# Held stores and a tick given out two parts per step, in a retention block with a gated feed-forward network

## The chip, the cores and the metric

The kernel runs on one core of a Trainium2 chip. The metric is the device time of one execution in microseconds (us); lower is better.

## The reference

```python
def reference(q, k, v, moe_w_gate, moe_w_val, moe_w_out):
    # q, k, v: (8, 8, 576, 64) float32; gates and values 512 x 1536, out 1536 x 512
    scores = (1 / np.sqrt(64)) * np.matmul(q, k.transpose(0, 1, 3, 2))
    gamma = 1.0 - 2.0 ** (-5.0 - np.arange(8))
    rel = pos[:, None] - pos[None, :]
    Dmat = np.where(rel >= 0, gamma[:, None, None] ** rel[None], 0.0)
    attn = np.matmul(scores * Dmat[None], v)
    x = attn.transpose(0, 2, 1, 3).reshape(4608, 512)      # tokens x (heads * 64)
    g = x @ w_gate
    return (g * (1.0 / (1.0 + np.exp(-g))) * (x @ w_val)) @ w_out
```

Everything is float32.

## The kernel before, in words

**The attention part** works on 32 pairs of heads (8 batches, 4 pairs each), in chunks of 128 positions with a running state. A pair passes through three *ticks*: tick t transposes q and k of pair t, computes scores and new states of pair t - 1, and the values of pair t - 2. `tick(t)` (L498 on) puts its matmuls out at once: new states (`mix`, L428, of v and the scaled k), own values (`xo`, L421), earlier values (L433, L438), scores (L444 and L447, of `qT` and `kT`). The rest goes into the list `pieces`, in this order: `keys`, which scales k by the decay of its position on ScalarE (two instructions, L408); `both`, which empties `mix` and `xo` into the activations x (L484, L478); three masked parts (L454 twice, and L459 to L462 together); two transposes on VectorE (L404, `qT` and then `kT`); and, in the later tiles, `next_load(t)`, which issues the load of pair t + 2. `go_on(n)` puts out the next n pieces. A tick first puts out whatever is left of the one before. `kT` and `ret` have one buffer, `qT` and the raw q and k have two, k in its natural order (`kn`) three, v four.

A load of a later pair is 14 transfers on SyncE's queue: four of q and four of k (L278), two of `kn` and two of v (L259), two of the last rows of v (L285). All transfers of the program share eight completion semaphores in turn, so that a transfer is issued only when the one eight places before it has landed.

**The feed-forward part** takes tokens in tiles of 1024 (the first has 512). The first tile uses plain matmuls: `up0(f)` for 12 blocks of hidden units, then `down0(f)` for the same 12 in the order of `down_order`, each four matmuls into four banks (L544). From the second tile on, the products go by a scheme with sums of weights, sums of activations and sums of results: each quarter has 26 products (`N`), in the order of the tables `UP` and `DOWN`. The second tile has 78 up steps (three quarters `qd` of 26), then 26 down steps; the same for the third, fourth and fifth tile.

The sums of the output weights are made once by GpSimd (L563 to L570) while the first tile runs: `out_sums` cuts the list `OUT_SUMS` into groups of three operands, 27 groups in all for three quarters. Each operand is stored to DRAM (L620, `dn<-rest`) by a transfer on SyncE's queue, or, for a group that is called `late`, on ScalarE's. Of late stores up to three wait in the list `waiting` before the oldest is put out:

```python
waiting.append((place.get(slot), lambda: queue.dma_start(...)))
stores_until(3 if late else 0)
```

A store whose operand is a plain piece of the weights has no place of its own (`None`), and `stores_until` then puts out all that wait. The groups of `up0(11)` (three) and of the first four down0 steps (one, one, one, two) are late. Sums have 18 places in SBUF, used again in turn.

In the down0 loop each step puts out its matmuls, `go_on(4)`, perhaps a tick (tick 10 after the second step, 11 after the fourth, 12 after the seventh, 13 after the ninth), and then its groups. Tick 13 is put out whole; ticks 10, 11 and 12 leave their pieces to later steps. Before the second tile, `out0` empties the four banks (VectorE copies A, B and C, L551), with sums of activations (L570 on VectorE) before and after.

In an up step of the second tile (`up_step` with `n == 1`, called `busy`): GpSimd makes sums of up weights for later steps (L570, and L733 after a negation on ScalarE, L732); eight matmuls go into a bank (L763); ScalarE's queue stores the operand for the later tiles (L766, `up<-arena`); at `i == 22` of the first two quarters `first_sums` makes the sums that the next quarter starts with, one of them on VectorE; at `i == 22` of the last quarter three fetches of stored down operands go out on SyncE's queue (L665, `arena<-dn`), and five more at `i == 25`; then `reads` empties the bank (ScalarE copies, L701; VectorE sums, L704; silu on ScalarE, L778; products on VectorE, L781 and L784); then `go_on(1)`. A bank is written again some three steps after it was filled.

The order on every engine and queue is the order of the calls. `merge` spreads ticks over steps: the first 26 up steps of the second tile run without ticks (two loads are put out among them), ticks 12 to 17 lie among the other 52 up steps, 8 or 9 steps each, and ticks 18 to 21 among the 26 down steps (L802), where `go_on(3)` follows each step.

Of the kernel before, what the change touches and what calls it, by code (L numbers as in the profile page):

```python
# [22 lines left out]
def tables(gamma, scale, P, D):  # L23
# [77 lines left out]
OUT_SUMS = [  # L101
    "14 | 10: add 8 4 5, add 9 2 3, nad 10 8 9",
    "2 | 11: add 11 0 1",
    "9 | 5: ",
    "19 | 9: neg 9 9",
    "15 | 12: sub 12 3 7",
    "0 | 11: sub 11 11 8",
    "1 | 13: sub 13 1 5",
    "6 | 10: add 10 0 2",
# [40 lines left out]
def kernel(  # L150
# [236 lines left out]
    def transposes(i):  # L387
        p = i % HP
        qk, kn, vt, last = loaded.pop(i)
        qT = qp.tile([P, S], F32, tag="qT", name="qT")  # L390
        st[i] = dict(qT=qT, kn=kn, v=vt, last=last)
        pieces = []
        if i < HP:

            for t, src, bank in ((qT, qk[0], bankA), (kT, kn, bankB)):
                for c in range(NFULL):
                    nc.tensor.transpose(bank[:, ts(c, P)], src[:, c].rearrange("p h d -> p (h d)"), ident)
                nc.scalar.copy(out=t[:, 0:CW], in_=bank)
            nc.tensor.transpose(bankC[:, 0:P], qk[1].rearrange("p h d -> p (h d)"), ident)
            for n, t in enumerate((qT, kT)):  # L400
                nc.scalar.copy(out=t[:, CW:S], in_=bankC[:, n * REM : (n + 1) * REM])
        else:
            for n, t in enumerate((qT, kT)):
                pieces.append(lambda n=n, t=t: nc.vector.transpose(out=t, in_=qk[:, n].rearrange("p j d -> p (j d)")))  # L404

        def keys():
            for hl in range(2):
                nc.scalar.activation(out=kn[:, :, hl, :], in_=kn[:, :, hl, :], func=AF.Copy,  # L408
                                     scale=key[:, 2 * p + hl : 2 * p + hl + 1])
            if i < RAWS:  # L410
                load_w(i)

        return [keys] + pieces
# [84 lines left out]
    def tick(t, lo=HP, hi=NP, spread=False, then=None):  # L498
        go_on(len(pieces))
        for fn, i in ((new_states, t - 1), (own_values, t - 2), (earlier_values, t - 2), (scores, t - 1)):  # L500
            if lo <= i < hi:
                fn(i)
        new = transposes(t) if lo <= t < hi else []
        pieces.extend(new[:1])
        if lo <= t - 2 < hi:
            pieces.extend(to_x(t - 2))
        if lo <= t - 1 < hi:
            pieces.extend(masked(t - 1))
        pieces.extend(new[1:])
        if then:  # L510
            pieces.append(then)
        if not spread:
            go_on(len(pieces))

    def go_on(n):
        for _ in range(min(n, len(pieces))):
            pieces.pop(0)()

    def needed(n):

        last = (min(starts[n] + TW, NT) - 1) // S
        return last * HP + HP - 1 + 3
# [55 lines left out]
    more_places = [rest[:, raw_at + TB * i : raw_at + TB * (i + 1)] for i in range(16) if i % 4]  # L578

    waiting = []  # L580

    def stores_until(left, place=None):
        while len(waiting) > left or any(p is place for p, _ in waiting):
            waiting.pop(0)[1]()
# [8 lines left out]
    def out_sums(qd):  # L593

        place = {}

        def view(s):
            return w_dn[:, qd, s // 2, s % 2] if s < 8 else place[s]

        def used(e):  # L600
            return [e[1]] if e[0] is None else [int(a) for a in e[1][2:]]

        def release(k):

            for s in list(place):
                for e in events[k + 1 :]:
                    if s in used(e):
                        break
                    if s == e[0]:
                        sum_places.append(place.pop(s))  # L610
                        break
                else:
                    sum_places.append(place.pop(s))

        def do(k, late):
            e = events[k]
            if e[0] is None:
                _, slot, i = e
                src, queue = view(slot), nc.scalar if late else nc.sync
                waiting.append((place.get(slot), lambda: queue.dma_start(out=dn_ops[i][:, qd * TB : (qd + 1) * TB], in_=src)))  # L620
                stores_until(3 if late else 0)
            else:
                new = sum_places.pop(0)
                stores_until(3, new)
                add(nc.gpsimd, e[1], view, new)
                if e[0] in place:
                    sum_places.append(place[e[0]])
                place[e[0]] = new
            release(k)

        r, ends = [], [k for k, e in enumerate(events) if e[0] is None]
        for g in range(0, N, 3):
            lo, hi = ends[g - 1] + 1 if g else 0, ends[min(g + 2, N - 1)] + 1

            def group(late=False, lo=lo, hi=hi):
                for k in range(lo, hi):
                    do(k, late)

            r.append(group)
        return r  # L640

    def up_view(qd):
        return lambda s: (w_up[:, qd, :, s // 2, s % 2, :] if s < 8
                          else extra[:, s - 8].rearrange("p (g x) -> p g x", g=2))
# [25 lines left out]
    def operand():  # L670
        m = used[0]
        used[0] += 1
        return ring[:, (m + 5) % 8]
# [46 lines left out]
    def x_sums(n, lo, hi, vector):  # L720
        for op in x_ops[lo:hi]:
            add(nc.vector if vector or op[0] == "nad" else nc.gpsimd, op, x_view(n))
# [24 lines left out]
    def up_step(n, qd, i):  # L747
        label, opens, xslot, _, wslot, _, ops = up[i]
        busy = n == 1
        if qd == 0:  # L750
            first = X_FIRST_OF_ALL if busy else X_FIRST
            x_sums(n, first + i, first + i + 1, busy)
        if busy:
            if i > 1:
                w_sums(qd, i)
            w = up_view(qd)(wslot)
        else:
            w = operand()[:, 0:512].rearrange("p (g x) -> p g x", g=2)
        rhs = x_view(n)(xslot)
        b = bank(label, i == 0)  # L760
        for gv in range(2):
            for c in range(2):
                nc.tensor.matmul(b[:, gv * TB : (gv + 1) * TB], w[:, gv, ts(c, P)], rhs[:, c, :],  # L763
                                 start=(opens and gv == 0 and c == 0), stop=(c == 1), skip_group_check=True)
        if busy:
            nc.scalar.dma_start(out=up_ops[qd][i].rearrange("p (g x) -> p g x", g=2), in_=w)  # L766
            if i == 22 and qd + 1 < NQ:
                first_sums(qd + 1)
            if qd + 1 == NQ and i >= 22:
                for _ in range(3 if i == 22 else 5 if i == N - 1 else 0):  # L770
                    fetch()
        else:
            fetch()

        def result(o, src, negative, vector):
            s = io[:, (silus[0] % 4) * TB : (silus[0] % 4 + 1) * TB]
            silus[0] += 1
            nc.scalar.activation(out=s, in_=src[:, 0:TB], func=AF.Silu, scale=-1.0 if negative else 1.0)  # L778
            dst = hid[:, qd, o // 4, o % 4]
            if negative:  # L780
                return lambda: nc.vector.scalar_tensor_tensor(out=dst, in0=src[:, TB : 2 * TB], scalar=-1.0, in1=s,  # L781
                                                              op0=ALU.mult, op1=ALU.mult)
            if vector:
                return lambda: nc.vector.tensor_tensor(out=dst, in0=src[:, TB : 2 * TB], in1=s, op=ALU.mult)  # L784
            nc.gpsimd.tensor_tensor(out=dst, in0=src[:, TB : 2 * TB], in1=s, op=ALU.mult)  # L785

        reads(ops, b, busy, result)
        if qd + 1 == NQ and i + 1 == N:
            while products:
                products.pop(0)[1]()  # L790
        go_on(1)

    def down_step(n, i):
        label, opens, slot, hops, ops = down[i]
# [50 lines left out]
    def next_load(t):  # L845
        if t + AHEAD < NP:
            load(t + AHEAD)
# [31 lines left out]
    for m, f in enumerate(down_order):  # L879
        down0(f)  # L880
        if m == 0:
            next_load(9)
        go_on(4)
        if m in tick_at:
            tick(tick_at[m], HP, FIRST, tick_at[m] + 1 < needed(1))
        if m == 8:
            first_sums(0)
        if m > 8:
            x_sums(1, 3 * (m - 9), min(3 * (m - 8), X_FIRST), True)
        for _ in range(min(1 if m < 3 else 2, len(groups))):  # L890
            groups.pop(0)[1](m < 4)
# [52 lines left out]
```

## Time and profile before

| what | value |
|---|---|
| median of 4 runs | 1112.57 us (1110.38 to 1117.3) |
| the profiled execution | 1112.69 us, span of its instructions 1111.0 us |
| TensorE (PE) busy | 1078.7 us, 97% |
| VectorE (DVE) busy | 653.2 us, 59% |
| GpSimd (POOL) busy | 404.6 us, 36% |
| ScalarE (ACT) busy | 257.8 us, 23% |
| mean granted TensorE clock | 0.992 |
| up0 and down0 of the first tile | up to 206 us of the span |
| up steps of the second tile | 206 to 366 us |

A line of the profile gives the kernel's line, the engine, the operation and what it writes and reads; `ACTq` and `SPq` are the queues on which ScalarE and SyncE issue transfers. In brackets stands how long the engine was idle before, and what ended the wait. A list of waits gives for each pair of waiting and awaited instruction the total in us, the number of times and the longest. In a table by stage each row is a stretch of time: its length, the busy time of PE, of PE's weight loads, DVE, ACT and POOL (with the number of instructions), the granted clock of TensorE, the busy share of the transfer engines and their GB/s.

### The profile page before, as it was taken

To read this page: it belongs to the slowest core of one execution; us is meant where nothing else is said; L and a number is where in the kernel's file an instruction comes from. 1 tells how busy PE (TensorE), PEld (TensorE's weight loads), DVE (VectorE), ACT (ScalarE), POOL (GpSimd) and SP (SyncE) were. 2 spreads that over 40 slices of the span, in tenths; PEclk is the share of its full clock that TensorE was granted. 3 is DMA by queue.
4 is the path that set the end of the run, shared out by engine and by line. 5 is a ranking of instruction groups with operands and counts; after the bars stand their busy time and mean duration, and the time that the engine had idled before them with its cause. 6 is when DMAs were issued, how large, how long until landed. Compare 5 with 4: busy or idle time off the path is not lost.

```text
span 1111.0 us, 17302 instructions
## 1 busy us (share of the span) xinstructions
PE 1078.7 (97%) x6372; PEld 884.5 (80%) x6372; DVE 653.2 (59%) x1063; ACT 257.8 (23%) x528; POOL 404.6 (36%) x355
## 2 busy tenths in 40 slices
PE   5999989999999899999999999999999999999998
PEld 4545446788878788888888888888888888888887
DVE  2698962976767765744536767444447455243654
ACT  3454500224232201112221110231321011322210
POOL 1002469366445402552214106622133176222504
PEclk9999999999999999999999999999999999999999
DMA  9989966656566877667467667654564555555653
GB/s 227 222 216 240 235 177 184 186 177 184 147 173 183 234 177 225 194 174 192 125 177 220 162 177 189 192 154 130 151 186 139 158 172 152 153 152 154 189 161 101
DMA packets 304196, 198.31 MB, mean 179 GB/s; under 512 B 219632, under 2 KB 247280, under 8 KB 304112
## 3 DMA queue, kind: packets, MB, share of 16 engines
q1 hardware_dynamic: 272512, 152.80, 53.2%
q10 hardware_dynamic: 31600, 44.41, 12.1%
q8 instruction: 51, 0.84, 0.3%
q14 instruction: 33, 0.27, 0.1%
HBM read 157.04 MB, written 40.11 MB: 177 GB/s over the span
## 4 chain that ended last, share of the span: by engine, by line
PE 79%; DVE 7%; DMA 5%; issue 3%; POOL 3%; ACT 2%; SPq 1%; ACTq 0%; DVEq 0%; POOLq 0%
PE bankE L763 11%; PE bankA L763 11%; PE bankC L763 10%; PE bankB L763 10%; PE bankE L802 6%; PE bankB L802 6%; PE bankC L802 6%; PE bankA L802 6%; PE sc L447 2%; DMA up<-arena 2%; PE xo L421 2%; PE xo L438 1%; DVE rest L373 1%; PE mix L428 1%; DVE rest L704 1%
## 5 line engine op out<-in xcount | busy, mean ns | idle before, releaser
L704 POOL TENSOR_TENSOR rest<-rest 128x512 f32<-128x512 f32 x56 | 79.1, 1417 | 313.8 <-DVE rest L704 288.7
L778 ACT ACTIVATE io<-rest 128x256 f32<-128x256 f32 x180 | 75.0, 417 | 357.0 <-DVE rest L704 311.0
L763 PE MATMUL bankC<-rest,arena 128*128 128x256 f32 x544 | 129.2, 380 | 0.5 <-DVE rest L704 0.5
L763 PE MATMUL bankA<-rest,arena 128*128 128x256 f32 x544 | 128.7, 379 | 0.0
L570 POOL TENSOR_TENSOR arena<-arena 128x512 f32<-128x512 f32 (+1 forms) x72 | 113.4, 1588 | 41.4 <-DMA up<-arena 30.6
L570 POOL TENSOR_TENSOR rest<-rest 128x256 f32<-128x256 f32 (+1 forms) x86 | 81.8, 972 | 122.4 <-DVE rest L375 94.0
L763 PE MATMUL bankE<-rest,arena 128*128 128x256 f32 x512 | 123.0, 384 | 0.0
L763 PE MATMUL bankB<-rest,arena 128*128 128x256 f32 x512 | 121.4, 380 | 0.8 <-DVE arena L781 0.8
L763 PEld LDWEIGHTS bankC<-rest,arena 128*128 128x128 f32 x544 | 102.8, 190 | 15.8 <-issue 1.3
L763 PEld LDWEIGHTS bankA<-rest,arena 128*128 128x128 f32 x544 | 103.2, 190 | 14.6 <-issue 0.5
L785 POOL TENSOR_TENSOR arena<-rest,io 128x256 f32<-128x256 f32 x72 | 51.8, 725 | 172.7 <-ACT io L778 172.7
L763 PEld LDWEIGHTS bankE<-rest,arena 128*128 128x128 f32 x512 | 98.0, 192 | 14.2 <-DVE rest L704 0.4
L763 PEld LDWEIGHTS bankB<-rest,arena 128*128 128x128 f32 x512 | 97.0, 190 | 14.8 <-DVE arena L781 1.2
L704 DVE TENSOR_TENSOR rest<-bankC,rest 128x512 f32<-128x512 f32 x72 | 48.9, 687 | 75.5 <-PE bankC L763 53.4
L704 DVE TENSOR_TENSOR rest<-bankE,rest 128x512 f32<-128x512 f32 x72 | 48.9, 687 | 75.0 <-PE bankE L763 56.0
L704 DVE TENSOR_TENSOR rest<-bankB,rest 128x512 f32<-128x512 f32 x72 | 48.8, 686 | 71.9 <-PE bankB L763 55.3
L704 DVE TENSOR_TENSOR rest<-bankA,rest 128x512 f32<-128x512 f32 x72 | 48.9, 687 | 67.2 <-PE bankA L763 48.9
L781 DVE SCALAR_TENSOR_TENSOR arena<-rest,io 128x256 f32<-128x256 f32 x84 | 55.2, 662 | 11.7 <-ACT io L778 11.7
L802 PE MATMUL bankB<-arena 128*128 128x256 f32 x252 | 58.2, 381 | 0.0
L802 PE MATMUL bankA<-arena 128*128 128x256 f32 x252 | 58.1, 380 | 0.0
L802 PE MATMUL bankC<-arena 128*128 128x256 f32 x252 | 58.0, 380 | 0.0
L802 PE MATMUL bankE<-arena 128*128 128x256 f32 x252 | 57.9, 379 | 0.0
(149 smaller groups left out, 1660.8 us busy)
## 6 DMA issues: line engine op xcount, KB each, us to landing
arena<-up SPq DMA_DIRECT2D x234, 256.0 KB, 2.7
arena<-dn SPq DMA_DIRECT2D x104, 384.0 KB, 3.5
up<-arena ACTq DMA_DIRECT2D x78, 256.0 KB, 2.7
out_dram<-rest SPq DMA_DIRECT2D x32, 256.0 KB, 3.5
qk<-in_q_dram SPq DMA_DIRECT2D x112, 72.0 KB, 3.2
qk<-in_k_dram SPq DMA_DIRECT2D x112, 72.0 KB, 3.1
v<-in_v_dram SPq DMA_DIRECT2D x62, 128.0 KB, 3.1
kn<-in_k_dram SPq DMA_DIRECT2D x58, 128.0 KB, 3.1
```

The costliest lines, as they stand in the source:

```text
L373: nc.vector.scalar_tensor_tensor(out=top, in0=top, scalar=-(1 << 31), in1=dst, op0=ALU.bitwise_and, op1=ALU.bitwise_or)
L421: nc.tensor.matmul(xo[half[hl], ts(c, P)], s["v"][:, c, hl, :], ret[:, hl, ts(c, P)], start=(c == 0), stop=(c == 0), skip_group_check=True)
L428: nc.tensor.matmul(z[half[hl], c], s["kn"][:, c, hl, :], s["v"][:, c, hl, :], start=True, stop=True)
L438: nc.tensor.matmul(o[half[hl]], state[half[hl], c - 1, :], s["qT"][half[hl], c * P : c * P + w], start=False, stop=True, skip_group_check= ...
L447: nc.tensor.matmul(sc[hl][:, ts(c, P)], kT[half[hl], ts(c, P)], qT[half[hl], ts(c, P)], start=True, stop=True)
L570: eng.tensor_tensor(out=dst, in0=srcs[0], in1=srcs[1], op=ALU.add if op[0] == "add" else ALU.subtract)
L704: eng.tensor_tensor(out=at(op[1]), in0=at(op[2]), in1=at(op[3]), op=ALU.add if op[0] == "add" else ALU.subtract)
L763: nc.tensor.matmul(b[:, gv * TB : (gv + 1) * TB], w[:, gv, ts(c, P)], rhs[:, c, :], start=(opens and gv == 0 and c == 0), stop=(c == 1), s ...
L778: nc.scalar.activation(out=s, in_=src[:, 0:TB], func=AF.Silu, scale=-1.0 if negative else 1.0)
L781: return lambda: nc.vector.scalar_tensor_tensor(out=dst, in0=src[:, TB : 2 * TB], scalar=-1.0, in1=s, op0=ALU.mult, op1=ALU.mult)
L785: nc.gpsimd.tensor_tensor(out=dst, in0=src[:, TB : 2 * TB], in1=s, op=ALU.mult)
L802: nc.tensor.matmul(b[:, m * TB : (m + 1) * TB], lhs[:, qd, ts(m, P)], w[:, qd], start=(opens and qd == 0 and m == 0), stop=(qd == NQ - 1), ...
```

## The change

Four edits. The number of late stores that may wait is no longer 3 but a variable that starts at 26; after the second down0 step and its tick it becomes 3 and the surplus is put out. After a tick in the down0 loop, one piece is put out at once: for ticks 10 and 11 that is the scaling of k, for tick 12 the emptying of `xo`; tick 13 has nothing left. In the up steps of the second tile two pieces are put out after each step instead of one. No instruction is added or removed.

```diff
@@ -578,6 +578,7 @@
     waiting = []
+    behind = [len(OUT_SUMS)]
 
     def stores_until(left, place=None):
@@ -618,10 +619,10 @@
                 waiting.append((place.get(slot), lambda: queue.dma_start(out=dn_ops[i][:, qd * TB : (qd + 1) * TB], in_=src)))
-                stores_until(3 if late else 0)
+                stores_until(behind[0] if late else 0)
             else:
                 new = sum_places.pop(0)
-                stores_until(3, new)
+                stores_until(behind[0], new)
                 add(nc.gpsimd, e[1], view, new)
@@ -788,7 +789,7 @@
             while products:
                 products.pop(0)[1]()
-        go_on(1)
+        go_on(2 if busy else 1)
 
     def down_step(n, i):
@@ -883,6 +884,11 @@
         go_on(4)
         if m in tick_at:
             tick(tick_at[m], HP, FIRST, tick_at[m] + 1 < needed(1))
+            go_on(1)
+        if m == 1:
+
+            behind[0] = 3
+            stores_until(3)
         if m == 8:
             first_sums(0)
```

## The prediction

> **What bounds the kernel now.** The page's first part is read first, to see whether any engine is full; then the list of TensorE's waits from 150 to 400 us, which is the stretch that the diff touches.
>
> ```profile
> PE 1078.7 (97%) x6372; PEld 884.5 (80%) x6372; DVE 653.2 (59%) x1063; ACT 257.8 (23%) x528; POOL 404.6 (36%) x355
> ...
> PE bankB L802 <- DMA arena<-dn: 4.1, 1, 4.1
> PE mix L428 <- ACT kn L408: 3.4, 1, 3.4
> PE mix L444 <- DVE kT L404: 2.4, 1, 2.4
> PE bankB L763 <- DVE arena L781: 0.8, 1, 0.8
> PE bankC L763 <- DVE rest L704: 0.5, 1, 0.5
> ```
>
> TensorE (PE) carries the span and stands still in few places: these five waits are 11.2 us. After 386 us it is never idle for more than a pipeline gap, so the change can move the end only through what it does to this list. The timelines of ScalarE (ACT), VectorE (DVE) and SyncE's queue (SP) show what stands before the three long waits, and the table by stage what follows them:
>
> ```profile
> 155.78 9.52 ACTq L620 DMA_DIRECT2D dn<-rest  x13
> 165.34 0.51 ACT L408 ACTIVATE kn<-kn,tab 128x256 f32<-128x256 f32 x1 [26.18 <-DMA qk<-in_k_dram]
> ...
> 303.13 1.74 DVE L570 TENSOR_TENSOR arena<-arena 128x512 f32<-128x512 f32 x1 [1.20 <-POOL arena L733]
> ...
> 309.23 0.76 DVE L404 STREAM_TRANSPOSE kT<-qk 128x576 f32<-128x576 f32 x1
> 310.05 0.33 PE L444 MATMUL mix<-qT,kT 64*64 64x64 f32 x4 [2.38 <-DVE kT L404]
> 311.44 3.60 PE L763 MATMUL bankE<-rest,arena 128*128 128x256 f32 x8
> ...
> 362.37 2.91 SPq L665 DMA_DIRECT2D arena<-dn  x3
> 369.87 3.42 SPq L278 DMA_DIRECT2D qk<-in_q_dram  x4
> 378.93 4.34 SPq L665 DMA_DIRECT2D arena<-dn  x8
> ```
> ```profile
> 165.91:172.34 6.43, 6.43 (x73) 5.75 (x73) 0.89 (x3) 0.34 (x1) 6.19 (x9) 0.58 0.58 174
> 182.84:186.57 3.73, 3.73 (x74) 3.37 (x73) 0.89 (x3) 0.00 (x0) 3.56 (x6) 1.00 0.59 194
> ```
>
> First, the k scaling of tick 10 (L408) stands behind 13 stores on ACT's queue; those wait for GpSimd (POOL), which makes the sums one by one from 152.61. TensorE, free at 162.48, waits 3.42 us, and tick 11 then takes 6.43 us at a granted clock of 0.58, where tick 12 takes 3.73 at 1.00. Second, the k transpose at 309.23 stands behind a weight sum that waited for POOL until 303.13, with multiplications after it. Third, eight fetches (L665) stand behind a load on SP (369.87 to 378.83).
>
> **The change part by part.** The sum is made against the profiled execution: 1112.69 us, of which the span is 1111.0. The median of the runs, 1112.57, lies 0.12 below it.
>
> *Held stores and scaling at once (down0 loop).* No arithmetic is added. By OUT_SUMS only the first three late stores still go out ahead of tick 10 (the third has no place of its own and pushes the two before it). The other ten of the 13 in the fence now stand behind the two scalings of tick 10. The three need a POOL sum that ends at 156.4, so the scaling runs near 158, and TensorE wants it at 162.48: wait gone, with 4 us of margin. Worth 3.42 + (6.43 - 3.73) = 6.1 us. The ten are paced by POOL and lose about 1 us.
>
> At tick 11 eight stores fall behind two scalings that wait for k of pair 11 (before: scaling ended at 176.70). Queued behind them are only these stores and, at 176.61 before, two weight negations that the second tile needs at 200. A store 0.5 us after another from 177.2, landing 2.1 us later, frees its place at 179.3; POOL writes that place again at 180.7. So POOL doesn't wait; without that margin it would, by a microsecond, and TensorE has 10 us of room for POOL's sums.
>
> What is late next? TensorE reaches tick 12 at 182.84 - 6.12 = 176.72. If the load of pair 11 keeps its times, its last v transfer (issued at 175.0, 3.1 to land) costs 1.4 us. But SP's waits show this load held 14.2 us by landings of those same stores; the last eight must now follow the scaling that needs the load, so the load can't wait for them any more. I take 0, and 1.4 as the other end. Then comes the second tile, wanted at 206.09 - 6.12 = 199.97, when bank A must have been copied out by DVE (done at 205.62, margin 0.47). Ahead of the copy stand nine sums: 0.69 us each alone, 1.64 (twice) beside a POOL instruction. POOL's chain doesn't move and runs until about 198, so four or five of the nine become slow instead of three: from 190.5 the copy ends at 200.9 or 201.9, a return of 0.9 to 1.9 (0 if none is slowed more). I take 1.4. Net: -4.7 us.
>
> The Trainium skill ("SBUF — State Buffer", "SBUF: two separate sides") speaks against the change here: the shared port is locked for a whole instruction. By it each overlapped sum would last up to 1.58 + 0.69 = 2.27 us, an estimate by which the return is 2.2; the row's 1.64 is less.
>
> *Two parts per step (second tile).* In the first 26 up steps there is nothing to give out. Ticks 12 to 17 cover 52 steps, 8 or 9 each, with up to eight parts: scaling (ACT), one part that empties xo, three masked parts, two transposes (DVE), the next load (14 transfers on SP). Counted from the tick, they end after the fourth step instead of the eighth; POOL's order is untouched. Tick 14's transposes leave the sixth and seventh step for the third and fourth, ahead of the weight sum at 303.13. That removes 2.38 and the slow step after it (314.87 - 311.44 - 1.73 = 1.70): 4.1 us. Against it: DVE has no gap from 293.2 to 301.9, and TensorE writes a bank again three steps after it was filled. Bank E's read ends at 297.39, wanted at 297.87; bank B's at 298.92, wanted at 299.59; bank A's margin is 0.6. With two masks ahead of it (1.2, less a gap of 0.1) bank E's read ends at 298.5: 0.6 late. Bank B's has one mask, the states (1.25) and a transpose (0.7) more ahead and ends at 301.3; wanted at 299.6 + 0.6, it is 1.1 late. Bank A's, with states and both transposes ahead, is 0.1 late. Return 1.8; between 0 and 2.7 (all that moved up). Net: -2.3 us. Ticks 12, 13, 15 and 16 fall into steps where DVE has gaps (2.66 at 270.8, 7.86 at 314.2, 2.48 at 332.1): nothing.
>
> The skill's "TensorE: Matmul & The Clock Gate" ("Part 1: The HAM clock gate") lets the clock fall only after an idle window of about 3.4 us. The row shows 0.54 granted after 2.38. By the page this part would bring 1.7 us less.
>
> *Tick 17's load and the fetches.* Here the change can lose. Tick 17's load is issued after the fourth step, so it passes the three fetches of the sixth (362.37), which fed the first three down steps; all eight fetches now stand behind it. By the same shifting of rows the k transpose that frees its buffer ends near 362.6, and TensorE comes 1.1 late to its first down step, at 371.2. The load's 14 transfers took 8.96 us here and 18.4 at the longest (328.44 to 346.80); most waits in the long ones are for up<-arena stores, of which four remain, so I take the row with the fewest: fetch issued at 371.6, 3.17 to land, 374.7. The first step then takes 4.51 at the low clock, as at 382.23, and three more 2.59 each: 387.0, where before the fifth step began at 386.75. So +0.3 us: the 4.06 wait doesn't go, it moves three steps forward. Ends: -5.1 (fetch in time, fifth step at 381.6) and +9.7 (load as long as 18.4).
>
> Sum: -4.7 - 2.3 + 0.3 = -6.7; 1112.69 - 6.7 = 1106.0, at the median 1105.9.
>
> **The rivals.** *Jam on SP:* the last load takes as long as the longest of the others, 18.4 us. Then +9.7 - 7.0 = +2.7: 1115.3, slower than before. It decides from 15.7 us on, where the third part has eaten the first two. For it: the five loads before this one took 13 to 18 us. Against: they ran beside eight or nine stores each, and the one that ran beside a single store took 8.96.
> *Given back:* the first two gains end at the next wait: pair 11's v costs 1.4, the shared port 1.9, the banks 2.7. Then -6.1 + 3.3 - 4.1 + 2.7 + 0.3 = -3.9: 1108.8. For it: margins of 0.5 to 0.7 us on DVE. Against: the load loses its reason to wait.
> *Fetches in time:* the load ends by 367.9, -5.1 in the third part: -12.1, 1100.6. Against: 14 issues of 0.5 us alone are 7 us, which from 362.6 is 369.6.
>
> **How the numbers follow.** Forecast 0.55, given back 0.22, jam 0.15, in time 0.08. A measurement of this kernel tells about 0.5% (5.6 us) from no change: faster is under 1107.0, slower over 1118.1. My forecast stands close to the line: with its unknown terms (0 to 1.9, 0 to 2.7, a load from 8 to 12 us) it lies between 1102.5 and 1109, and 0.44 of its 0.55 is faster. With the fetches in time: 0.52. The jam reaches past 1118 only when further stores queue up behind it, and 0.1 of its 0.15 counts as slower for that. The rest, 0.38, is no change. The range goes from the fetches in time to the jam, 1100.0 to 1115.3, and leaves out what lies past either.
>
> **What would show it.** Right: no wait of mix L428 on kn L408 near 162; tick 11 in 3.7 us at clock 1.00; a short wait for bank A at the second tile's start; no wait on kT near 305, but waits of up to 1 us of L763 on DVE L704 before it; the load's L278 ahead of all L665 on SP, and the wait for arena<-dn at the first down step instead of the fourth. Wrong: the first down step starts before 372 or after 380 on this profile's scale; a new wait of over 1 us at tick 12; POOL waiting for dn<-rest between 158 and 192.

## The result and the profile after

The changed kernel takes 1111.61 us (median of 54 runs, 1108.86 to 1118.96) against 1114.11 us for the kernel before in the same comparison (78 runs): a ratio of 0.9983, 95% interval 0.9974 to 0.9991. By the ratio that is 1.9 us less, between 1.0 and 2.9. The direction of the forecast was right; of the 6.7 us that it summed up, some three tenths came. The time lies inside the forecast's range, but in the class "no change" (within 0.5%), which had 0.38 against 0.52 for faster.

The profiled execution has a span of 1109.4 us. The first line is from the page's busy times; the rest is its list of TensorE's waits from 150 to 400 us, with total, number and longest. Line numbers behind the edits are one to six higher: L764 is the up step's product (L763 before), L803 the down step's (L802), L705 the reads of the banks (L704), L666 the fetches (L665).

```profile
PE 1076.3 (97%) x6372; PEld 881.0 (79%) x6372; DVE 654.3 (59%) x1063; ACT 257.5 (23%) x528; POOL 404.8 (36%) x355
```
```profile
PE bankA L803 <- DMA arena<-dn: 5.1, 1, 5.1
PE bankB L764 <- DVE rest L705: 1.5, 2, 0.8
PE bankA L764 <- DVE rest L551: 1.0, 1, 1.0
PE bankE L764 <- DVE rest L705: 1.0, 2, 0.7
PE bankB L764 <- DVE arena L782: 0.8, 1, 0.8
PE bankA L764 <- DVE rest L705: 0.7, 1, 0.7
PE bankC L764 <- DVE rest L705: 0.5, 1, 0.5
PE bankE L764 <- POOL arena L734: 0.3, 1, 0.3
PE bankC L764 <- POOL arena L734: 0.3, 1, 0.3
```

The waits for `kn` (3.4) and `kT` (2.4) are gone, and so is the one of 4.1 at the fourth down step. In their place stand one of 5.1 for the first fetch, one of 1.0 for bank A's copy, five short ones for bank reads (B twice, E twice, A) and two of 0.3 for GpSimd; bank B's 0.8 for L782 and bank C's 0.5 stood in the kernel before too. The next rows are a table by stage, for tick 11 and for the first down step, and TensorE's and SP's timelines at the end of the up steps:

```profile
163.21:166.94 3.73, 3.73 (x73) 3.37 (x72) 0.89 (x3) 0.00 (x0) 3.56 (x6) 1.00 0.68 190
...
372.02:377.08 5.06, 5.06 (x13) 4.11 (x14) 3.18 (x5) 0.00 (x0) 0.47 (x1) 0.55 0.99 371
```
```profile
372.02 5.06 PE L803 MATMUL bankA<-arena 128*128 128x256 f32 x12 [5.11 <-DMA arena<-dn]
376.92 2.75 PE L803 MATMUL bankB<-arena 128*128 128x256 f32 x12
```
```profile
357.60 1.96 SPq L278 DMA_DIRECT2D qk<-in_q_dram  x4
359.61 5.15 SPq L278 DMA_DIRECT2D qk<-in_k_dram  x4
...
367.06 1.11 SPq L285 DMA_DIRECT2D vl<-in_v_dram  x2
368.28 14.33 SPq L666 DMA_DIRECT2D arena<-dn  x11
```

Tick 11 runs in 3.73 us at full clock, as forecast. Tick 17's load holds SP from 357.60 to 368.18, all fetches stand behind it, and TensorE, done with tick 18 at 366.9, waits until 372.02; its first step then runs at a granted clock of 0.55.

TensorE executes the same 6372 matmuls in the same order in every kernel here, so two profiles can be laid side by side: the start of a matmul in one, less the start of the same matmul in the kernel before. The table gives what each stretch gained (minus) or lost, in us, and on its left how far the two profiles already stood apart at tick 10. That offset runs from -1.5 to +4.2 us over the thirteen profiles, although no edit moves work that runs ahead of tick 10; I take it as the scatter of the single execution (whose cause was not looked for; most of it is there by 44 us), and the stretches to its right leave it out. The last column has the measured times, as a ratio. Where a sum and the times differ, as for held stores alone, the times decide, since a sum is one execution.

| kernel | offset at tick 10 | tick 10 to second tile | to the step after tick 15 | to tick 18 | to the fifth down step | sum from tick 10 | ratio to before (95%) |
|---|---|---|---|---|---|---|---|
| the change | +0.80 | -5.04 | -1.40 | +2.35 | +1.39 | -2.70 | 0.9983 (0.9974 to 0.9991) |
| first part alone | -1.52 | -3.97 | -0.06 | +0.71 | -0.46 | -3.78 | 0.9956 (0.9938 to 0.9973) |
| second part alone | -0.27 | -2.53 | -1.73 | +2.35 | +2.19 | +0.28 | 1.0002 (0.9982 to 1.0023) |
| one part after tick 17 | +1.91 | -5.04 | -1.10 | -0.20 | -0.95 | -7.29 | 0.9943 (0.9924 to 0.9961) |
| load behind fetches | +2.68 | -4.87 | -1.28 | +2.35 | -5.99 | -9.79 | 0.9915 (0.9891 to 0.9940) |
| load and pace moved | +4.19 | -4.70 | -1.38 | -0.20 | -5.98 | -12.26 | 0.9907 (0.9881 to 0.9933) |
| scaling at once alone | +1.47 | -5.03 | +0.56 | +0.70 | -0.48 | -4.25 | 0.9957 (0.9936 to 0.9978) |
| held stores alone | +3.44 | -0.16 | -1.89 | +0.70 | -1.24 | -2.59 | 1.0008 (0.9990 to 1.0026) |
| four earlier stores out | -0.56 | -4.37 | -0.23 | +2.35 | +0.36 | -1.89 | 0.9984 (0.9966 to 1.0001) |
| last four stores out | -0.75 | -4.51 | -1.32 | +2.34 | -1.20 | -4.69 | 0.9964 (0.9948 to 0.9980) |
| pairs late in tick 14 only | +1.63 | -4.63 | -2.62 | +0.71 | -5.99 | -12.53 | 0.9898 (0.9882 to 0.9913) |
| first part, load behind | +0.22 | -4.89 | +0.36 | +0.70 | -5.99 | -9.82 | 0.9917 (0.9895 to 0.9939) |
| before, load behind | -0.75 | +0.11 | -0.22 | +0.70 | -5.99 | -5.40 | 0.9952 (0.9936 to 0.9968) |

In the first row stand the three steps of the forecast: -5.04 (forecast -4.7), -1.40 (-2.3), and +2.35 + 1.39 = +3.74 (+0.3). The theory to test is that the first two parts work as forecast and that the third, the fetches behind the load, was sized too small. Its rival is that any gain is taken back by the next thing that is late.

### The profile page after: what moved, and what is told of

Read it like the earlier page. It is cut to its first block, busy times and chain, and to the rows that moved or that the text cites. A ratio compares the mean times of both kernels' runs of the same rounds, so it can differ in the third digit from the quotient of the medians.

```text
span 1109.4 us, 17314 instructions
## 1 busy us (share of the span) xinstructions
PE 1076.3 (97%) x6372; PEld 881.0 (79%) x6372; DVE 654.3 (59%) x1063; ACT 257.5 (23%) x528; POOL 404.8 (36%) x355
## 4 chain that ended last, share of the span: by engine, by line
PE 80%; DVE 8%; DMA 5%; issue 3%; SPq 2%; POOL 1%; ACT 1%; ACTq 0%; DVEq 0%; POOLq 0%
PE bankC L764 11%; PE bankE L764 11%; PE bankA L764 11%; PE bankB L764 10%; PE bankA L803 6%; PE bankB L803 6%; PE bankC L803 6%; PE bankE L803 6%; PE sc L447 2%; PE xo L421 2%; PE xo L438 1%; DVE rest L705 1%; DVE rest L570 1%; PE mix L428 1%; DMA qk<-in_q_dram 1%
## 5 line engine op out<-in xcount | busy, mean ns | idle before, releaser
L705 POOL TENSOR_TENSOR rest<-rest 128x512 f32<-128x512 f32 x56 | 79.1, 1418 | 318.0 <-DVE rest L705 299.4
L764 PE MATMUL bankA<-rest,arena 128*128 128x256 f32 x544 | 128.9, 380 | 1.7 <-DVE rest L551 1.0
L764 PE MATMUL bankC<-rest,arena 128*128 128x256 f32 x544 | 129.3, 380 | 0.5 <-DVE rest L705 0.5
L764 PE MATMUL bankE<-rest,arena 128*128 128x256 f32 x512 | 121.5, 380 | 1.1 <-DVE rest L705 1.0
L764 PE MATMUL bankB<-rest,arena 128*128 128x256 f32 x512 | 121.4, 380 | 0.8 <-DVE arena L782 0.8
L764 PEld LDWEIGHTS bankA<-rest,arena 128*128 128x128 f32 x544 | 102.9, 190 | 17.2 <-issue 3.2
L764 PEld LDWEIGHTS bankC<-rest,arena 128*128 128x128 f32 x544 | 102.7, 190 | 16.1 <-issue 1.2
L764 PEld LDWEIGHTS bankE<-rest,arena 128*128 128x128 f32 x512 | 96.8, 190 | 15.5 <-issue 1.6
L764 PEld LDWEIGHTS bankB<-rest,arena 128*128 128x128 f32 x512 | 97.0, 190 | 14.8 <-DVE arena L782 1.2
L705 DVE TENSOR_TENSOR rest<-bankC,rest 128x512 f32<-128x512 f32 x72 | 48.9, 688 | 78.1 <-PE bankC L764 55.7
L705 DVE TENSOR_TENSOR rest<-bankE,rest 128x512 f32<-128x512 f32 x72 | 48.9, 687 | 72.1 <-PE bankE L764 53.4
L705 DVE TENSOR_TENSOR rest<-bankB,rest 128x512 f32<-128x512 f32 x72 | 48.8, 686 | 70.6 <-PE bankB L764 54.0
L705 DVE TENSOR_TENSOR rest<-bankA,rest 128x512 f32<-128x512 f32 x72 | 48.9, 687 | 68.9 <-PE bankA L764 50.7
L803 PE MATMUL bankA<-arena 128*128 128x256 f32 x252 | 60.3, 391 | 5.1 <-DMA arena<-dn 5.1
L782 DVE SCALAR_TENSOR_TENSOR arena<-rest,io 128x256 f32<-128x256 f32 x84 | 55.9, 670 | 10.6 <-ACT io L779 10.6
L803 PEld LDWEIGHTS bankA<-arena 128*128 128x128 f32 x252 | 49.2, 196 | 12.5 <-DVE state L462 5.3
L803 PE MATMUL bankB<-arena 128*128 128x256 f32 x252 | 58.2, 381 | 0.0
L803 PE MATMUL bankC<-arena 128*128 128x256 f32 x252 | 58.0, 380 | 0.0
```

Source lines behind the costliest of these rows:

```text
L705: eng.tensor_tensor(out=at(op[1]), in0=at(op[2]), in1=at(op[3]), op=ALU.add if op[0] == "add" else ALU.subtract)
L803: nc.tensor.matmul(b[:, m * TB : (m + 1) * TB], lhs[:, qd, ts(m, P)], w[:, qd], start=(opens and qd == 0 and m == 0), stop=(qd == NQ - 1), ...
```

## The experiments

**The parts alone.** The first part alone keeps `go_on(1)` in the up steps; the second part alone is the kernel before with this one edit:

```diff
-        go_on(1)
+        go_on(2 if busy else 1)
```

> Only the first part: stores of sums held, k scaled at once after a tick; the second tile's up steps give out one part each, as before. Theory (each part keeps its own price; the loss sits in the last load and the fetches): the wait for k near 162 and the half-clock tick go, bank A costs about 1 us, the k transpose near 305 costs its 2.4 + 1.7 us again, the three fetches go out ahead of the load: 4 to 5.5 us less than the kernel before, more than with both parts. Rival (a gain of any kind is eaten at the down steps, since fetches and loads have times of their own): 0 to 2 us less, about as with both parts.

> Only the second part: two parts per up step, stores and scaling as before. Theory: -1.4 from the k transpose at tick 14 less the bank reads that come later, +3.6 at the first down step, where the fetches stand behind the load: about 2 us more than the kernel before (0 to +3). Rival (the two parts cover different waits and the first part's gain is the one that is lost): 1 to 3 us less.

The first part alone measured 0.9956, 4.9 us less: more than the whole change, so the second part takes back some 3 us of what the first brings. The second part alone measured 1.0002 (0.9982 to 1.0023): no gain, and an interval of -2.0 to +2.6 us that holds both no change and the 2 us of loss expected. Its row shows the parts. It loses 2.35 + 2.19 = 4.54 at the end of the quarter and gains 1.73 at the k transpose, which is the loss expected; but its profile shows another -2.53 before the second tile, where nothing is edited. Of that, 2.30 is the clock after the wait for `kn`, on which the last section has more. Whether this explains the measured times as well isn't shown: it is seen in one execution.

**The last quarter's order.** Three kernels change only what stands around tick 17's load. The first returns to one part per step there, the second leaves the pace and issues this load behind the eight fetches, the third does both.

```diff
-        go_on(2 if busy else 1)
+        go_on(2 if busy and not (qd + 1 == NQ and i >= 17) else 1)
```
```diff
                 for _ in range(3 if i == 22 else 5 if i == N - 1 else 0):
                     fetch()
+            if qd + 1 == NQ and i == N - 1:
+                load(19)
...
-        tick(t, FIRST, NP, True, lambda: next_load(t))
+        tick(t, FIRST, NP, True, None if t == 17 else lambda: next_load(t))
```

> Both parts, but after tick 17 the up steps give out one part each again, so that three fetches go out ahead of its load, and the reads of the banks come as early as before. Theory: the 2.35 us of bank waits in that interval go, and the wait of the fourth down step returns with about 4 us and a slow step, as in the kernel before: 5 to 6 us less than before, so 3 to 4 less than with the change. Rival (the fetches' landing is set by the stores and the memory, not by their place behind the load): within 1 us of the change.

> The whole change, but tick 17's load (14 transfers) is issued after the eight fetches instead of ahead of them. Theory: the 5.1 us wait of the first down step and the 2.5 us of its half clock go, nothing takes their place: 8 to 9.5 us less than the kernel before, 6.5 to 7.5 less than with the change. Rival (the load is then late itself: tick 19's transposes stand on VectorE ahead of the reads of the banks, and TensorE waits there): a gain of under 4 us on the change, with a wait of TensorE on VectorE between 385 and 400.

> The load behind the eight fetches, and after tick 17 one part per up step again. Theory (the two losses of the last quarter are separate: 2.35 us of bank waits between ticks 17 and 18, and the wait and the half clock at the first down step): both go, 11 to 12.5 us less than the kernel before, 2 to 2.5 less than with the load alone moved. Rival (the bank waits hide another wait, as the 4.06 us of the fourth down step hid others): as with the load alone moved, 9 to 10 us less.

One part after tick 17: 0.9943, 6.4 us less than before; the rival is out. The bank waits of the last interval are gone (-0.20 instead of +2.35), and the wait is back at the fourth down step (3.1 us). With the load behind the fetches: 0.9915, 9.5 us less. TensorE's waits from 150 to 400 us in that kernel:

```profile
PE bankB L764 <- DVE rest L705: 1.5, 2, 0.8
PE bankA L764 <- DVE rest L551: 1.2, 1, 1.2
PE bankE L764 <- DVE rest L705: 1.1, 2, 0.7
PE bankB L764 <- DVE arena L784: 0.8, 1, 0.8
PE bankA L764 <- DVE rest L705: 0.7, 1, 0.7
PE bankC L764 <- DVE rest L705: 0.5, 1, 0.5
PE bankE L764 <- POOL arena L734: 0.3, 1, 0.3
PE bankC L764 <- POOL arena L734: 0.3, 1, 0.3
```

No wait for a fetch is left, none of the down steps up to the fifth is slow, and the load, now issued from 372.45, delays nothing up to 400 us: the stretch to the fifth down step gains 5.99 on the kernel before, where it lost 1.39. With both moved: 0.9907, 10.4 us less by the ratio (7.5 to 13.2) and 12.26 by the table. The table's order, and its two separate terms (2.35 and 5.99), are as expected; the 10.4 lies between the 11 to 12.5 expected and the rival's 9 to 10, and by the ratios the two kernels can't be told apart.

**The load alone.** The same edit of the load on the kernel before, and with the first part:

> The kernel before with one edit: tick 17's load behind the eight fetches. Theory: the 4.06 us wait of the fourth down step and its half clock (some 1.5 us) go, all else stays: 5 to 6 us less than the kernel before. Rival (the load itself is late then, and VectorE's transposes of tick 19 hold up the banks): 0 to 2 us less, with a wait of TensorE on VectorE between 385 and 400.

> The first part and the load behind the eight fetches; one part per up step everywhere, as before. Theory (the parts add): the k transpose near 305 costs its 2.4 + 1.7 us again, nothing is lost to the banks; the wait of the fourth down step is gone: 9 to 10.5 us less than the kernel before, 1.5 to 2.5 more than with load and pace both moved. Rival (without the wait for fetches the two parts per step are worth nothing, since something later takes them): the same time as both moved within 1 us.

On the kernel before it measured 0.9952, 5.3 us less, and 5.40 in the table: a move that the change didn't make brings about as much as its whole first part (4.9). With the first part it is 0.9917. By the table that kernel (-9.82) equals the whole change with the load moved (-9.79): over the second tile two parts per step gain 1.28 up to the step after tick 15 and lose 2.35 from there to tick 18, where one part loses 0.36 and 0.70. The sums are equal, and the times too (0.9917 and 0.9915), so even without the fetches two parts everywhere are worth nothing that shows. Against load and pace both moved it stands 2.4 us behind in the table, within the 1.5 to 2.5 expected; by the ratios the two can't be told apart either.

**Why the load was long.** In the trace of the change four of its transfers wait for landings of up<-arena stores at 363.50, 364.43, 365.42 and 366.43; the first two hold SP for 1.4 and 0.6 us, the other two land just as SP comes to their transfer. Two kernels leave four such stores out (the later tiles then fetch operands that were not stored).

```diff
-            nc.scalar.dma_start(out=up_ops[qd][i].rearrange("p (g x) -> p g x", g=2), in_=w)
+            if not (qd + 1 == NQ and i >= 22):
+                nc.scalar.dma_start(out=up_ops[qd][i].rearrange("p (g x) -> p g x", g=2), in_=w)
+            if qd == 0 and i >= 22:
+                nc.scalar.dma_start(out=up_ops[NQ - 1][i].rearrange("p (g x) -> p g x", g=2), in_=w)
```

> The whole change, but the four stores of the steps after tick 17 are left out (four others, of the first quarter, are written in their place some 90 us earlier), so that nothing lands late beside the load. Theory (the load's transfers wait for a count that the stores' landings share): the load takes 7.2 to 8 us on SP instead of 10.6 and shows no wait for up<-arena; the first down step comes 2.5 to 3.5 us earlier, and the time is 4.5 to 5.5 us less than the kernel before. Rival (the load's own transfers set its pace): the load keeps 10 us or more, and the time is within 1 us of the change's.

> The whole change, but the stores of the last four up steps are left out (four others, of the first quarter, are written in their place some 90 us earlier): these are the ones that were issued beside tick 17's load and whose landings it waited for at 363.5 to 366.4 in the trace of the change. Theory (those four waits made the load longer than the 8.96 us of the step that was predicted): the load takes 7.2 to 8.6 us on SP, the first fetch goes out 2 to 3.4 us earlier, and so does the fifth down step; 4 to 5.5 us less than the kernel before. Rival (the load's own transfers set its pace): 10 us or more, and within 1 us of the change's time.

The first, with steps 17 to 20 (`17 <= i <= 20`) in the place of `i >= 22`, missed its mark: these stores had landed before the load began. The load still waits for four stores, those of the last steps, from 358.08 to 368.58, and the time is that of the change (0.9984). The second leaves those out. SP's timeline in it:

```profile
356.65 1.96 SPq L278 DMA_DIRECT2D qk<-in_q_dram  x4
358.65 3.57 SPq L278 DMA_DIRECT2D qk<-in_k_dram  x4
362.32 0.98 SPq L259 DMA_DIRECT2D kn<-in_k_dram  x2
363.40 1.01 SPq L259 DMA_DIRECT2D v<-in_v_dram  x2
364.51 1.11 SPq L285 DMA_DIRECT2D vl<-in_v_dram  x2
365.73 13.34 SPq L666 DMA_DIRECT2D arena<-dn  x11
```

From 356.65 to 365.62 are 8.97 us, the length that the forecast took (8.96), against 10.58. The first fetch goes out 9.08 after the load's start instead of 10.68, the wait at the first down step is 3.3 instead of 5.1, and the time 0.9964, 4.0 us less than before, the near end of what was expected. So the waits for these four stores made the load 1.6 us longer than the row that it was sized by. The load itself is not as short as the 7.2 to 8.6 us expected, and the first fetch comes 1.6 us earlier on the scale of before, not 2 to 3.4: one of the 14 transfers held SP for 1.94 us, where most take 0.5. Why is not known. That the length equals the forecast's row is partly chance, since that row is made up differently: a wait of 0.5 for a store and one transfer of 1.46.

**Which half of the first part.** One kernel gives the scaling out at once and holds no stores (`behind = [3]`, no release after the second step); the other holds the stores and leaves out the `go_on(1)` after a tick.

> Only the extra part after a tick (k scaled at once); no store is held back, up steps as before. Nine stores instead of 13 stand ahead of the scaling of tick 10, the ninth paced by the sum that POOL ends three sums earlier, some 3 to 4 us. Theory (the place of the scaling is what counts, the held stores only add margin): the wait of 3.4 us shrinks to 0 to 0.6 and the clock stays, 4 to 5.5 us less than the kernel before, as with the whole first part. Rival (the held stores carry it): a wait of 2 us or more and the half clock stay, 0 to 1.5 us less.

> Only the held stores; no part is given out directly after a tick, up steps as before. The ten held stores are let go right after tick 10, and the scaling is given out a step later, behind them. Theory (the place of the scaling counts): the wait for k near 162 stays, 0 to 1 us less than the kernel before. Rival (the stores are what held ACT up and their being late is enough): 4 to 5.5 us less.

The scaling at once measured 0.9957, as the whole first part; held stores alone 1.0008. ScalarE's timelines show it, first of the scaling at once, then of the held stores:

```profile
156.68 6.07 ACTq L621 DMA_DIRECT2D dn<-rest  x9
162.79 0.51 ACT L408 ACTIVATE kn<-kn,tab 128x256 f32<-128x256 f32 x1 [22.64 <-DMA dn<-rest]
```
```profile
158.75 9.52 ACTq L621 DMA_DIRECT2D dn<-rest  x13
168.31 0.51 ACT L408 ACTIVATE kn<-kn,tab 128x256 f32<-128x256 f32 x1 [25.77 <-DMA qk<-in_k_dram]
```

Nine stores ahead of the scaling are few enough, if only just: its second instruction ends at 163.70, TensorE starts tick 11 at 163.88, and there is no wait for `kn`. With the stores held and let go ahead of the scaling, 13 stand in front of it and TensorE waits 2.95 us. Holding the stores added margin and no gain in time.

**A version that beats both.** The load behind the fetches, and two parts per step only in the last six steps of tick 14's interval:

```diff
-        go_on(2 if busy else 1)
+        go_on(2 if busy and qd == 1 and i >= 20 else 1)
```

> As with load and pace both moved, but two parts are given out only in the last six steps of tick 14's interval; everywhere else in the second tile one per step. Theory (two parts serve only that one k transpose; in the other intervals they do nothing or cost): the time of both moved within 1 us, with the bank waits between 294 and 303 at 1 us or less if the later start spares banks E and B, so 0 to 1.5 less. Rival (the k transpose then still comes too late, behind the weight sum that waits for POOL): a wait for kT of 1 to 2.4 us near 305 and 2 to 4 us more than both moved.

It measured 1102.0 us, 0.9898 (0.9882 to 0.9913): 11.4 us less than the kernel before, and clear of the change (0.9974 to 0.9991); by the ratios it can't be told from load and pace both moved. Its waits from 150 to 400 us:

```profile
PE bankA L764 <- DVE rest L551: 1.4, 1, 1.4
PE mix L444 <- DVE kT L404: 0.8, 1, 0.8
PE bankB L764 <- DVE arena L784: 0.8, 1, 0.8
PE bankA L764 <- DVE rest L705: 0.6, 1, 0.6
PE bankC L764 <- DVE rest L705: 0.5, 1, 0.5
PE bankE L764 <- DVE rest L705: 0.4, 1, 0.4
PE bankC L764 <- POOL arena L734: 0.3, 1, 0.3
```

The k transpose near 305 is in time, bank B waits no more for L705 (0.75 at each of ticks 14 and 17 before this edit), and the stretch to the step after tick 15 gains 2.62 instead of 1.38. The wait of 0.8 for `kT` is another one, at tick 17. All kernels with one part in tick 16's interval show it (the +0.7 to tick 18), though the profiled execution of the kernel before doesn't. The two kernels with two parts in tick 16's interval and one after tick 17 lack it (-0.20), so two parts may serve there too; together with this version that wasn't run.

## Why the prediction was right, and where it failed

*First part: right.* -5.04 and, alone, -3.97 to -5.03, for a forecast of -4.7. The wait and the slow tick (6.43 to 3.73) are gone, for the reason given: only three stores go out ahead of the scaling, which starts at 157.88 for the forecast's 158.

```profile
155.94 1.89 ACTq L621 DMA_DIRECT2D dn<-rest  x3
157.88 0.51 ACT L408 ACTIVATE kn<-kn,tab 128x256 f32<-128x256 f32 x1 [18.51 <-DMA dn<-rest]
```

The return at bank A's copy, forecast at 1.4 within 0 to 1.9, was 1.0 in the change and 1.0 to 2.1 in the other kernels with this part: five of the nine sums ahead of the copy ran slowed in the change, seven in the first part alone, which passes the forecast's far end. The Trainium skill's "SBUF — State Buffer" ("SBUF: two separate sides") was the source of an estimate of up to 2.27 for a slowed sum; the longest in these profiles is 1.75. The return of 2.2 put down to it lies above all that were measured, the 2.1 closely; one or two more sums at 1.58 would in fact make it 1.6 to 3.2. Tick 12 shows no wait for pair 11's v, and POOL works without a wait from 152.76 to 198, both as forecast. What the forecast did not say is that its two edits are not equal: the scaling alone does it.

*Second part: right in kind, 0.9 short.* The wait and slow step at tick 14 went (from 285.40 to 305.08 and on to 314.87 on the scale of before: +2.52, then -4.23). The return is the first of these numbers, 2.5 for a forecast of 1.8 with 2.7 as its far end. Of the three waits that it named two came at tick 14, E 0.70 and B 0.75; for bank A there is none, and bank C waits 0.32 for POOL's L734, which it had not named. They are 1.77 together, almost the forecast's 1.8; the other 0.75 stands in no wait, some 0.25 for each of the three interruptions. The remaining 0.3 of the shortfall is a wait of 0.27 for bank E near 218, which isn't this part's: scaling at once alone has it (0.52), the second part alone doesn't.

*Third part: this step failed.* It was put at +0.3 and measured +3.74, which is 3.4 of the 4.0 us that separate the forecast's sum (-6.7) from the table's (-2.70). Its mechanism is confirmed: the load is ahead of the fetches, the wait moves from the fourth to the first down step, and a load behind the fetches removes it wholly. The mis-sized terms are these. "TensorE comes 1.1 late" to the first down step: 2.35, because in this interval too two banks, here A and B, are read late and POOL is waited for (0.71, 0.75 and 0.33). That alone would cost nothing, since the fetch ends later still. "8.96, the row with the fewest": the load took 10.58, because that row ran beside one store and this load beside four. The fetch went out 0.1 after it and took 3.60 to land, not 3.17. The k transpose ended 0.6 later than forecast (357.58 + 5.64 = 363.2). On the scale of before the first down step starts at 372.02 + 5.64 = 377.7, not 374.7: 0.6 + 1.6 + 0.1 + 0.4 are 2.7 of these 3.0, and 0.14 is the gap from landing to the first matmul. The first step took 5.06 at the low clock instead of 4.51: 0.55 more. Together 3.5, for a measured difference of 3.74 - 0.3 = 3.4.

The forecast had the counter-argument in hand: it wrote that four stores remained, and then took the row that had met one. The rows that it had, 8.96 to 18.4, held the measured 10.58; the forecast took the shortest of them.

Of the rivals, "jam" was right that stores lengthen the load, but by 1.6 us and not by 9.4, a sixth of its size. "Given back" was nearest in time (1108.8), in part by luck: its returns came to 1.0 of 1.9 at the copy, 2.5 of 2.7 at the banks and none for v, and the loss at the fetches, which it held at 0.3 like the forecast, made up the rest. Of the signs listed, all on the right side were seen; the test of the third part was too loose, since a first down step at 377.7 lies inside its 372 to 380 and the gain was nonetheless lost.

## What to carry to other kernels

When parts are given out sooner, look at the last of them: it is a block of transfers on a queue, and what it passes on that queue may be wanted first. Here 14 transfers that TensorE needs only at tick 20 (412.02) passed three fetches, the first of which it needed at 366.9, and putting them behind cost nothing that the profile shows and brought more than the change. Size a transfer block by the row that met the same neighbours, not by the one with the shortest time. Give out two parts where one piece is late, not everywhere: each piece moved up stands ahead of a bank's read.

## What the runs showed of the hardware

*The clock after a wait is not decided by the wait's length alone.* The tables by stage, first of the second part alone (tick 11 after a wait of 3.19 us), then of held stores alone (tick 11 after 2.95 us, and the step after the k transpose, after 2.37 us), then of the kernel before with the load behind (the same step after 2.38 us):

```profile
165.41:169.54 4.13, 4.06 (x73) 3.56 (x73) 0.89 (x3) 0.35 (x1) 3.96 (x6) 1.00 0.55 156
```
```profile
168.87:175.61 6.74, 6.74 (x72) 6.06 (x72) 0.89 (x3) 0.35 (x1) 6.49 (x10) 0.55 0.57 169
313.08:316.26 3.18, 3.18 (x28) 2.80 (x29) 2.88 (x7) 0.83 (x2) 0.00 (x0) 1.00 0.68 147
```
```profile
309.22:314.01 4.79, 4.79 (x28) 4.11 (x29) 3.85 (x8) 0.83 (x2) 0.00 (x0) 0.64 0.80 185
```

After 3.19 us the clock stayed at 1.00, after 2.95 it was 0.55; after 2.37 it stayed, after 2.38 it was 0.64. The same work took 4.13 or 6.74 us, and 3.18 or 4.79. In five of the six profiles with this wait for `kT` of 2.36 to 2.38 the step was slow (4.79 to 4.87). So the slow step behind a wait of 2.4 to 3.2 us is a term with two values, and a sum that counts it in full (as the forecast did with 1.70, behind 2.38) takes one of two outcomes as sure. What decides between them was not tested. The Trainium skill's "TensorE: Matmul & The Clock Gate" ("Part 1: The HAM clock gate") has the gate look at a window that runs freely, so that the moment of a wait counts beside its length: that agrees with these rows. That a whole window of about 3.4 us must be idle does not: the clock fell after 2.38.

*A queue can be held by landings of another queue's transfers.* SP's load stood still for stores that ScalarE had issued, though it neither reads nor writes what they store; with the stores gone it took 8.97 us instead of 10.58. In the trace all transfers of this program count on eight completion semaphores, and each of the waiting ones has the same as the store that it waited for: the store issued at 358.95 landed at 363.50, and the transfer eight places behind it went out at 363.52.
